# Single-tile slots by column parts, and the ranking and scores of the last tiles in another order

## The chip, the cores and the metric

The kernel runs on one core of a Trainium2 chip. The metric is the device time of one execution in microseconds (us). Matrix products run on TensorE (PE in the profile; PEld is its weight load), element-wise work on VectorE (DVE), ScalarE (ACT) and GpSimd (POOL), and SyncE (SP) issues most transfers. Each engine works through its own queue in order; between queues, an instruction waits for the semaphores of those whose data or buffers it needs.

## The reference

All in float32, with random inputs of fixed sizes:

```python
def _attn_ref(r, k, v, w, u):            # B 2, H 8, S 768, D 48
    for t in range(S):
        cur = np.einsum('bhd,bhe->bhde', u[None] * kt, vt)
        y[:, :, t] = np.einsum('bhd,bhde->bhe', rt, state + cur)
        state = wt[:, :, :, None] * state + np.einsum('bhd,bhe->bhde', kt, vt)

def _moe_ref(x, w_gate, w1, w2):         # N 1536, D 384, E 8, F 1024
    P = np.exp(logits - logits.max())    # logits = x @ w_gate
    for _ in range(8):
        P /= P.sum(1, keepdims=True) + 1e-09
        P /= P.sum(0, keepdims=True) + 1e-09
        P *= N / E
    for e in range(E):
        out += P[:, e:e + 1] * (np.maximum(x @ w1[e], 0.0) @ w2[e])

def _moe2_ref(x, expert_emb, tau, w1, w2):   # same sizes
    logits = normalised(x) @ normalised(expert_emb).T / tau
    expert_idx = np.argmax(logits, axis=1)
    gate_w = softmax(logits)[np.arange(N), expert_idx]
    for e in range(E):
        mask = expert_idx == e
        out[mask] = gate_w[mask, None] * (np.maximum(x[mask] @ w1[e], 0.0) @ w2[e])

def reference(**kwargs):
    x = rows of _attn_ref                # 1536 rows of 384
    return _moe2_ref(x=_moe_ref(x=x, **moe), **moe2)
```

## The kernel before

The 1536 rows are 12 tiles of 128. Each float32 product is made of three matmuls of rounded operands (high by high, high by low, low by high); `hh` and `hl` are the high and low half of a hidden value, and a weight split (`wA`, `wB`) takes ScalarE for the high half (L252) and VectorE for the low half (L258).

The work goes in stages: the recurrence (to about 100 us), the first mixture with eight experts on all rows (to about 870 us), and the top-1 mixture in slots, each of which takes the rows of one expert (up to two tiles of 128, gathered from a table `xs` in memory into which each row was scattered), to about 1035 us. The last expert of the first mixture runs in four units of three tiles, `m1_unit(E - 1, 0/3/6/9)`. A unit is a list of pieces: eight hidden pieces (nine matmuls, L274) and then product pieces (L294 to L296). Behind each piece the lists given to `run` put side work, so the position in a list sets the place in every engine's queue. There is no planner behind it: what is issued later stands later in the queue.

The side work of these units prepares the top-1 mixture. As the add L804 (`acc`) finishes a tile's row, ScalarE copies it to PSUM (L885) and sums its squares (L877, `sumsq`), VectorE makes five of the eight scores (`route_dots`, L731: a product with accumulated sum and a read of that sum), and GpSimd and ScalarE make the others (L738, L724). Then, for groups of tiles (`route`): the one-hot of the best expert (`route_arg`, L916 to L921), the root chain for the norm (`gate_a`, L817 to L832), positions within the expert (`route_pos`: L935 matmuls on TensorE, then L937 to L944), running counts (`route_cum`, `cum`, L951), the gate (`gate_b`, `gate_c`, L975 to L988), and the scatter (`route_rows`, L958). Tiles 10 and 11 get their scores on TensorE instead, by transposes of the finished row (`route_tr`, L893) and matmuls (`route_mm`, L904). `choose` takes the fullest expert after three tiles for slot 0; `order` (L1010 on), after nine tiles, ranks the other experts into slots 1 to 7.

Ten slots (`m2_slot`) follow, the last ones for what does not fit. Slots 3, 5 and 7 (`TURN`) hold one tile, and their hidden pieces run turned: `turned_pieces` takes the rows as stationary operand, makes the hidden values of all 1024 columns in three slabs over the contraction into three banks, and transposes them (L341) for the second product. The second tile of every slot from the first on stands under a condition on a bit of a word. While one slot runs, the splits of the next slot's weights stand in its side work (`its`, `at_`), and `m2_xT(s + 1)` transposes the next slot's gathered rows (L707).

Of the kernel before, what the change touches and what calls it, by code (L numbers as in the profile page):

```python
# [8 lines left out]
F32 = mybir.dt.float32  # L9
# [10 lines left out]
def rwkv_sinkhorn_moe_top1_moe(  # L20
# [291 lines left out]
    def turned_pieces(g, xh, xl, finish, own=False):  # L312


        w1h, w1l, _, _ = wt[g]
        parts = [range(0, 3), range(3, 6), range(6, 8)]
        hts, box, banks, hid = [], [], [], []

        def slab(kk):
            if kk == 0:  # L320
                banks.extend(ps() for _ in parts)
            mm = [(xh, w1h), (xh, w1l), (xl, w1h)]
            for i, (a, b) in enumerate(mm):
                for p, fs in zip(banks, parts):
                    n = len(fs) * 128
                    cs = slice(fs[0] * 128, fs[0] * 128 + n)
                    nc.tensor.matmul(
                        p[:, 0:n], a[:, kk, :], b[:, kk, cs],
                        start=(kk == 0 and i == 0), stop=(kk == KD - 1 and i == 2),
                    )  # L330
            if kk == KD - 1:
                for i, fs in enumerate(parts):
                    n = len(fs) * 128
                    hid.append(hp.tile([128, 384], F32, tag="hh", name="hid") if own else acc[:, 8 + i])
                    nc.scalar.activation(out=hid[i][:, 0:n], in_=banks[i][:, 0:n], func=AF.Relu)

        def turn(i):
            t, n = ps(), len(parts[i]) * 128
            for q in range(len(parts[i])):
                cs = slice(q * 128, (q + 1) * 128)  # L340
                nc.tensor.transpose(t[:, cs], hid[i][:, cs], ident)  # L341
            hh = hp.tile([128, 384], F32R, tag="hh", name="hh")
            hl = hp.tile([128, 384], F32R, tag="hl", name="hl")
            nc.scalar.activation(out=hh[:, 0:n], in_=t[:, 0:n], func=AF.Copy)  # L344
            nc.vector.tensor_tensor(out=hl[:, 0:n], in0=t[:, 0:n], in1=hh[:, 0:n].bitcast(F32), op=ALU.subtract)
            for q in range(len(parts[i])):
                cs = slice(q * 128, (q + 1) * 128)
                hts.append((hh[:, cs], hl[:, cs]))

        return [lambda k=k: slab(k) for k in range(KD)] + [lambda i=i: turn(i) for i in range(3)] + [  # L350
            lambda q=q: y_part(g, q, 4, 0, hts, box) for q in range(3)
        ] + [lambda: finish(0, y_part(g, 3, 4, 0, hts, box))]

    S_t = {}
    B21, B22, B31, B32, B11, T3, T1, T2, T4 = range(9)
# [525 lines left out]
    def route_dots(t, es, n_pool):  # L881
        x = acc[:, t, 0:DM]
        if es[0] == 0:
            xp, junk = rr["xp", t] = ps(), ps()
            nc.scalar.activation(out=xp[:, 0:DM], in_=x, func=AF.Copy)  # L885
            sumsq(t, junk)
        dots(lg[:, t, :], x, *rr["xp", t], lambda e: en[:, e, :], es, n_pool, late)

    def route_tr(t):
        x1 = acc[:, t, 0:DM]  # L890
# [104 lines left out]
    def choose():  # L995
# [8 lines left out]
        nc.vector.tensor_copy(first, est[:, 0:1])  # L1004
        nc.vector.tensor_scalar(oe, wdesc, m, None, op0=ALU.is_equal)

    def order():
# [8 lines left out]
        nc.vector.tensor_scalar(mk, kio, est[:, 0:1], full, op0=ALU.is_ge, op1=ALU.mult)  # L1016
        b = small[0].tile([128, NS], F32, tag="b", name="b")
        nc.vector.tensor_tensor(b, kio, mk, ALU.add)
        nc.vector.tensor_scalar(ids[:, E - 1:E], est[:, 0:1], 0.0, None, op0=ALU.add)
        nf = sp.tile([128, E], F32, tag="fl", name="nf")  # L1020
        nc.vector.tensor_scalar(nf[:, 0:1], full, -1.0, 1.0, op0=ALU.mult, op1=ALU.add)
        nc.vector.tensor_scalar_add(nf[:, 1:2], est[:, 0:1], -float(E - 1))
        nc.vector.scalar_tensor_tensor(
            out=b[:, E:E + 1], in0=nf[:, 1:2], scalar=nf[:, 0:1], in1=b[:, E:E + 1], op0=ALU.mult, op1=ALU.add
        )

        key = sp.tile([128, E], F32, tag="jk", name="key")
        nc.vector.scalar_tensor_tensor(out=key, in0=p, scalar=float(E), in1=wdesc, op0=ALU.mult, op1=ALU.add)
        nc.vector.scalar_tensor_tensor(out=key, in0=oe, scalar=float(OOB), in1=key, op0=ALU.mult, op1=ALU.add)
        sq = [128, E, E]  # L1030
        c = sp.tile([128, NTILE, E], F32, tag="tmp", name="rank")[:, 0:E]
        nc.vector.tensor_tensor(
            c, key.unsqueeze(1).to_broadcast(sq), key.unsqueeze(2).to_broadcast(sq), ALU.is_gt
        )
        nc.vector.tensor_reduce(f, c, axis=AX.X, op=ALU.add)
        se = [128, E - 1, E]
        d = c[:, 0:E - 1]
        c = sp.tile([128, NTILE, E], F32, tag="tl", name="at")[:, 0:E - 1]
        nc.vector.tensor_tensor(
            c, f.unsqueeze(1).to_broadcast(se), want.unsqueeze(2).to_broadcast(se), ALU.is_equal  # L1040
        )
        nc.vector.tensor_tensor(d, c, wdesc.unsqueeze(1).to_broadcast(se), ALU.mult)
        nc.vector.tensor_reduce(b[:, 1:E], d, axis=AX.X, op=ALU.add)
        nc.vector.tensor_scalar(b[:, 1:E], b[:, 1:E], -1.0, float(E), op0=ALU.mult, op1=ALU.add)
        nc.vector.tensor_scalar_min(blk, b, float(E + NOV - 1))
        nc.vector.tensor_tensor(c, c, pow2.unsqueeze(2).to_broadcast(se), ALU.mult)
        nc.vector.tensor_reduce(wtab, c.rearrange("p s e -> p e s"), axis=AX.X, op=ALU.add)
        nc.vector.tensor_scalar_mul(nf[:, 0:1], nf[:, 0:1], float(1 << E))
        nc.vector.scalar_tensor_tensor(out=wtab, in0=oe, scalar=nf[:, 0:1], in1=wtab, op0=ALU.mult, op1=ALU.add)
# [154 lines left out]
    with tc.manual_schedule():  # L1204
# [156 lines left out]

        def m2_slot(s, extra=()):
            its = w_items(E + s + 1)
            turned = s in TURN
            side = [[] for _ in range(KF + 8)]
            if s and s + 2 < NS:
                side[0].append(lambda: m2_load(s + 2))
            if s and s + 1 < NS:
                side[2].append(lambda: m2_xT(s + 1))
            if s == 1:  # L1370
                side[0].append(overflow_word)
                side[KF + 1].append(overflow_rows)
# [1 line left out]
                for i, j in enumerate((3, 5, 7)):  # L1374
                    side[j].append(lambda t=3 * (s - 2) + i: over_scatter(t))
            if turned:
                its = its[KD:]
                at_ = (0, 1, 3, 5)
            elif s + 1 in TURN:
                its = its + w_items(E + s + 2)[:KD]  # L1380
                at_ = (0, 1, 3, 4, 5, 6, 7, KF, KF + 1, KF + 1)
            else:
                at_ = (5, 6, 7, 8, 9, 15, 15) if s == 0 else (1, 4, 6, KF, KF, KF + 1, KF + 1)
            if its:
                for j, it in zip(at_, its):
                    side[j].append(it)
# [3 lines left out]
            if s == 0:  # L1390
                run(pieces, side)
                return
            n = 10 if turned else KF + 2
            run(pieces[:n], side)
            if s == 1:
                word.append(nc.values_load(word_t[0:1, 0:1], min_val=0, max_val=(NS + 1) * (1 << NS) - 1))
            with tc.If(((word[0] >> s) & 1) > 0):
                for pc in pieces[n:]:
                    pc()

# [43 lines left out]
        def load_to(g):  # L1444
# [95 lines left out]
```

## Time and profile before

| | |
|---|---|
| median of 3 runs | 1045.8 us (1045.76 to 1046.46) |
| profiled execution | 1045.61 us, span 1043.9 us |
| mean granted TensorE clock | 0.993 |
| busy: TensorE, weight load | 1015.2 us (97%), 995.0 us (95%) |
| busy: VectorE, ScalarE, GpSimd | 700.9 us (67%), 413.9 us (40%), 207.1 us (20%) |

The span runs from the first to the last instruction; the profiled execution's time also holds what lies around it. With TensorE busy for 97%, an idle stretch on it is time that the program loses, and an idle stretch elsewhere is not, unless TensorE waits for that engine.

### The profile page before, as it was taken

What the parts mean: (1) busy time and instruction counts of PE and PEld (TensorE: products, weight loads), DVE (VectorE), ACT (ScalarE), POOL (GpSimd) and SP (SyncE); (2) the same over time, 40 slices, a digit from 0 to 9 for tenths busy, and PEclk for the clock granted to TensorE, in tenths of its full rate; (3) what the DMA queues carried; (4) which work ended last, traced back from release to release, by engine and by line L of the source; (5) the groups of instructions that cost most, each with busy time, mean ns of one, the idle gap of its engine ahead of it and who ended that gap; (6) DMA issues with size and microseconds to landing.
All of it is one profiled execution on the core that took longest, in us unless ns stands there. A gap on an engine that the chain in (4) does not pass through costs nothing.

```text
span 1043.9 us, 19767 instructions
## 1 busy us (share of the span) xinstructions
PE 1015.2 (97%) x7714; PEld 995.0 (95%) x7714; DVE 700.9 (67%) x1413; ACT 413.9 (40%) x851; POOL 207.1 (20%) x393
## 2 busy tenths in 40 slices
PE   7999999999999999999999999999999998999996
PEld 6899999999999999999999999999999997999996
DVE  7998858666655665566456556655547787977764
ACT  3323234535432342333234323433434545566553
POOL 3211152040100010002001000000234663144101
PEclk9999999999999999999999999999999999999998
DMA  8435201201220122021011100120011314888762
GB/s 248 120 109 158 84 10 46 76 1 31 84 78 1 61 84 77 10 88 50 7 31 61 31 1 31 61 77 15 19 59 37 100 38 139 293 300 281 244 207 68
DMA packets 55783, 91.71 MB, mean 88 GB/s; under 512 B 5355, under 2 KB 47191, under 8 KB 55554
## 3 DMA queue, kind: packets, MB, share of 16 engines
q1 hardware_dynamic: 53056, 85.60, 26.4%
q0 software_dynamic: 2624, 4.75, 1.2%
q8 instruction: 64, 1.05, 0.4%
q14 instruction: 37, 0.30, 0.1%
q10 hardware_dynamic: 2, 0.00, 0.0%
HBM read 80.42 MB, written 13.28 MB: 90 GB/s over the span
## 4 chain that ended last, share of the span: by engine, by line
PE 67%; issue 14%; DVE 9%; POOL 5%; ACT 2%; DMA 1%; POOLq 0%; DVEq 0%; SPq 0%; ACTq 0%
PE ps L502 29%; PE ps L427 24%; PE ps L274 6%; PE ps L294 2%; PE ps L296 2%; PE ps L295 1%; POOL tmp L738 1%; DVE ps L731 1%; POOL xs L1136 1%; PE ps L631 1%; POOL out_dram L1182 1%; DVE hl L443 1%; DVE keep L438 1%; PE ps L663 1%; ACT hh L442 1%
## 5 line engine op out<-in xcount | busy, mean ns | idle before, releaser
L502 PE MATMUL ps<-wA,hh 128*128 128x384 f32 x864 | 221.6, 337 | 0.4 <-ACT hh L442 0.4
L502 PEld LDWEIGHTS ps<-wA,hh 128*128 128x128 f32 x864 | 156.7, 188 | 1.2 <-ACT hh L442 1.2
L506 DVE SCALAR_TENSOR_TENSOR acc<-ps,Pe,acc 128x384 f32<-128x384 f32 x144 | 88.7, 616 | 101.7 <-PE ps L502 101.3
L433 ACT ACTIVATE keep<-ps 128x384 f32<-128x384 f32 x144 | 70.2, 488 | 208.9 <-PE ps L427 207.1
L502 PE MATMUL ps<-wA,hl 128*128 128x384 f32 x432 | 145.6, 337 | 0.2
L443 DVE SCALAR_TENSOR_TENSOR hl<-keep,hh 128x384 fp32r<-128x384 f32 x144 | 81.7, 567 | 92.0 <-ACT hh L442 92.0
L438 DVE TENSOR_TENSOR keep<-ps,keep 128x384 f32<-128x384 f32 x192 | 106.3, 554 | 40.2 <-PE ps L427 34.2
L232 POOL TENSOR_TENSOR stage<-stage 128x128 f32<-128x128 f32 x96 | 49.3, 535 | 416.4 <-DMA stage<-in_moe_w_dram 414.5
L442 ACT ACTIVATE hh<-keep 128x384 fp32r<-128x384 f32 x144 | 75.4, 524 | 123.8 <-DVE keep L438 123.6
L427 PE MATMUL ps<-xTAhi,wA 128*128 128x384 f32 x396 | 101.6, 338 | 0.2 <-ACT keep L433 0.2
L279 ACT ACTIVATE hh<-ps 128x256 fp32r<-128x256 f32 (+1 forms) x128 | 53.0, 416 | 91.5 <-PE ps L274 72.9
L294 PE MATMUL ps<-wA,hh 128*128 128x384 f32 x248 | 85.1, 343 | 1.8 <-ACT hh L344 1.7
L296 PE MATMUL ps<-wA,hl 128*128 128x384 f32 x248 | 83.6, 337 | 0.4
L295 PE MATMUL ps<-wA,hh 128*128 128x384 f32 x248 | 83.3, 336 | 0.0
L502 PEld LDWEIGHTS ps<-wA,hl 128*128 128x128 f32 x432 | 81.1, 188 | 1.2 <-DVE hl L443 1.2
L258 DVE TENSOR_TENSOR wA<-stage,wA 128x768 fp32r<-128x768 f32 (+2 forms) x65 | 72.5, 1118 | 4.9 <-ACT wA L252 4.6
L280 DVE SCALAR_TENSOR_TENSOR hl<-ps,hh 128x256 fp32r<-128x256 f32 (+1 forms) x128 | 57.5, 460 | 26.6 <-ACT hh L279 26.2
L502 PE MATMUL ps<-slot,hh 128*128 128x384 f32 x288 | 74.2, 339 | 0.0
L427 PEld LDWEIGHTS ps<-xTAhi,wA 128*128 128x128 f32 x396 | 71.7, 188 | 0.5 <-ACT keep L433 0.5
L252 ACT ACTIVATE wA<-stage 128x768 fp32r<-128x768 f32 (+2 forms) x65 | 60.5, 956 | 26.6 <-POOL stage L232 26.0
L427 PE MATMUL ps<-xTAlo,wA 128*128 128x384 f32 x198 | 66.7, 337 | 0.0
L274 PE MATMUL ps<-xTAhi,wA 128*128 128x256 f32 (+1 forms) x336 | 58.3, 309 | 0.0
(332 smaller groups left out, 2093.1 us busy)
## 6 DMA issues: line engine op xcount, KB each, us to landing
stage<-in_moe_w_dram SPq DMA_DIRECT2D x55, 384.0 KB
stage<-in_moe_w_dram SPq DMA_DIRECT2D x19, 512.0 KB
en<-in_moe_w_dram SPq DMA_DIRECT2D x17, 512.0 KB
stage<-in_moe_w_dram SPq DMA_DIRECT2D x28, 256.0 KB
rkv<-in_rkv_dram SPq DMA_DIRECT2D x12, 576.0 KB
en<-in_moe_w_dram SPq DMA_DIRECT2D x18, 384.0 KB
rk<-in_wrk_dram SPq DMA_DIRECT2D x24, 192.0 KB
stage<-in_moe_w_dram SPq DMA_DIRECT2D x28, 128.0 KB
```

Of the source, the lines that this page charges most:

```text
L258: eng.tensor_tensor(out=lo, in0=src, in1=hi.bitcast(F32), op=ALU.subtract)
L274: nc.tensor.matmul(p[:, 0:n], w1_of(g, kk, f)[lo], b[:, kk, :], start=(i == 0), stop=(i == len(mm) - 1))
L294: nc.tensor.matmul(p, hh[:, ts], w2h, start=(f == 0), stop=False)
L295: nc.tensor.matmul(p, hh[:, ts], w2l, start=False, stop=False)
L296: nc.tensor.matmul(p, hl[:, ts], w2h, start=False, stop=(f == KF - 1))
L427: nc.tensor.matmul(t, w, x, start=first_mm and q == 0, stop=q == n - 1, skip_group_check=True,)
L433: nc.scalar.activation(out=t, in_=st_[i][bank][:, 0:384], func=AF.Copy)
L438: nc.vector.tensor_tensor(t, st_[i][bank][:, 0:384], t, ALU.add)
L442: nc.scalar.activation(out=hh, in_=src, func=AF.Relu)
L443: nc.vector.scalar_tensor_tensor(out=hl, in0=src, scalar=0.0, in1=hh.bitcast(F32), op0=ALU.max, op1=ALU.subtract)
L502: nc.tensor.matmul(p, h[:, ts], w, start=n == 0, stop=n == len(mm) - 1)
L506: nc.vector.scalar_tensor_tensor(out=a, in0=p, scalar=P[:, t, e:e + 1], in1=a, op0=ALU.mult, op1=ALU.add)
```

## The change

Five edits, in the diff below.

1. In the single-tile slots, `part(i)` makes the hidden columns of one part with all nine matmuls of the contraction, and the list becomes part 0, part 1, transposes 0, part 2, transposes 1, product 0, transposes 2, products 1 to 3. The two first weight splits in the slot (`pre`) are issued ahead of the pieces, two more at pieces 2 and 6, and the next slot's row transposes behind piece 5.
2. `sumsq` of a tile is issued behind the tile's last scores.
3. The ranking is split: `rank_a`, `rank_b` and `rank_c` (counts of the first six tiles, keys, ranks, tables) stand in the third unit at sides 6, 7 and 9; what is left in `order` is ten instructions.
4. In the third and fourth units: the scatters of tiles 3 to 5 stand behind the scores of tile 6, two weight splits move into slot 0, the add of tile 10 comes between the scores of tile 9, and the root chain of tiles 10 and 11 is on GpSimd. In slot 0 the steps of tiles 10 and 11 spread over pieces 1 to 6 and the next splits come a piece later.
5. The condition is `word & (1 << s)` instead of `(word >> s) & 1`.

```diff
+        def part(i):
+            p, fs = ps(), parts[i]
+            n = len(fs) * 128
+            cs = slice(fs[0] * 128, fs[0] * 128 + n)
+            mm = [(a, b, kk) for a, b in ((xh, w1h), (xh, w1l), (xl, w1h)) for kk in range(KD)]
+            for q, (a, b, kk) in enumerate(mm):
+                nc.tensor.matmul(p[:, 0:n], a[:, kk, :], b[:, kk, cs], start=(q == 0), stop=(q == len(mm) - 1))
+            hid.append(hp.tile([128, 384], F32, tag="hh", name="hid"))
+            nc.scalar.activation(out=hid[i][:, 0:n], in_=p[:, 0:n], func=AF.Relu)
...
-        return [lambda k=k: slab(k) for k in range(KD)] + [lambda i=i: turn(i) for i in range(3)] + [
-            lambda q=q: y_part(g, q, 4, 0, hts, box) for q in range(3)
-        ] + [lambda: finish(0, y_part(g, 3, 4, 0, hts, box))]
+        if own:
+            pa = [lambda i=i: part(i) for i in range(3)]
+            return [pa[0], pa[1], ts[0], pa[2], ts[1], ys[0], ts[2]] + ys[1:]
+        return [lambda k=k: slab(k) for k in range(KD)] + ts + ys
...
-            sumsq(t, junk)
         dots(lg[:, t, :], x, *rr["xp", t], lambda e: en[:, e, :], es, n_pool, late)
+        if es[-1] == E - 1:
+            sumsq(t, rr["xp", t][1])
...
+    def rank_a():
+        p = counts()
+        key = rr["key"] = small[0].tile([128, E], F32, tag="sc1", name="key")
+        nc.vector.scalar_tensor_tensor(out=key, in0=p, scalar=float(E), in1=wdesc, op0=ALU.mult, op1=ALU.add)
+        nc.vector.scalar_tensor_tensor(out=key, in0=oe, scalar=float(OOB), in1=key, op0=ALU.mult, op1=ALU.add)
+        sq = [128, E, E]
+        p = rr["rank"] = ps()
+        c = p[:, 0:E * E].rearrange("p (a b) -> p a b", b=E)
+        nc.vector.tensor_tensor(
+            c, key.unsqueeze(1).to_broadcast(sq), key.unsqueeze(2).to_broadcast(sq), ALU.is_gt
+        )
+        nc.vector.tensor_reduce(key, c, axis=AX.X, op=ALU.add)
...
             if s and s + 1 < NS:
-                side[2].append(lambda: m2_xT(s + 1))
+                side[5 if turned else 2].append(lambda: m2_xT(s + 1))
...
             if turned:
-                its = its[KD:]
-                at_ = (0, 1, 3, 5)
+                its, pre = its[KD + 2:], its[KD:KD + 2]
+                at_ = (2, 6)
...
-                at_ = (5, 6, 7, 8, 9, 15, 15) if s == 0 else (1, 4, 6, KF, KF, KF + 1, KF + 1)
+                at_ = (6, 7, 8, 9, 10, 15, 15) if s == 0 else (1, 4, 6, KF, KF, KF + 1, KF + 1)
...
-            with tc.If(((word[0] >> s) & 1) > 0):
+            with tc.If((word[0] & (1 << s)) > 0):
...
-            dt[0:1], dt[1:2], dt[2:3], rt[0:2], its[1:2], [], [rt[2]], [rt[3]],
-            its[2:3], rt[4:], dots_of(6), its[3:4], dots_of(7), its[4:5],
+            dt[0:1], dt[1:2], dt[2:3], rt[0:2], its[1:2], [], [rt[2], rank_a], [rt[3], rank_b],
+            its[2:3], [rt[4], rank_c], dots_of(6), its[3:4] + [rt[5]], dots_of(7), its[4:5],
...
-        ra, rb = route(8, 10, nc.gpsimd), route(10, 12, nc.vector)
+        ra, rb = route(8, 10, nc.gpsimd), route(10, 12, nc.gpsimd)
...
-            [order, lambda: load_to(E + SURE)], its[5:6], [], [], dots_of(9)[0:2], dots_of(9)[2:], [ra[1]], [ra[0]],
+            [order, lambda: load_to(E + SURE)], [], [], [], dots_of(9)[0:1], [], [], dots_of(9)[1:] + [ra[1], ra[0]],
...
-            (0, [lambda: route_mm(10), lambda: route_tr(11), ra[4], more_stages]), (1, [lambda: route_mm(11), ra[5], rb[0], rb[1]] + its[6:7]),
-            (3, rb[2:4]), (4, rb[4:]), (5, [lambda: m2_load(1)]), (6, [lambda: m2_load(2)]),
+            (0, [lambda: route_mm(10), lambda: route_tr(11), ra[4], more_stages]),
+            (1, [lambda: route_mm(11), ra[5], rb[1], rb[0]]), (2, its[5:6]),
+            (3, rb[2:3]), (4, its[6:7]), (5, rb[3:4]), (6, rb[4:] + [lambda: m2_load(1)]), (7, [lambda: m2_load(2)]),
```

TensorE in the third unit, before, at the end of the position matmuls of tiles 3 to 5 (L935) and the eighth hidden piece (L274):

```order
L935 MATMUL ps<-oh,oneb 128x8
L935 LDWEIGHTS oneb
L935 MATMUL ps<-oh,oneb 128x8
L935 LDWEIGHTS oneb
L935 MATMUL ps<-cum,oneb 128x8
L274 MATMUL ps<-xTAhi,wA 128x384 x6
L274 MATMUL ps<-xTAlo,wA 128x384 x3
L294 MATMUL ps<-wA,hh 128x384
```

The same place after the change, where line numbers are higher by 15 (L950 are the position matmuls, L1007 the counts):

```order
L950 MATMUL ps<-oh,oneb 128x8
L950 LDWEIGHTS oneb
L950 MATMUL ps<-oh,oneb 128x8
L950 LDWEIGHTS oneb
L950 MATMUL ps<-cum,oneb 128x8
L1007 LDWEIGHTS oneb
L1007 MATMUL ps<-cum,oneb 128x8
L274 MATMUL ps<-xTAhi,wA 128x384 x6
L274 MATMUL ps<-xTAlo,wA 128x384 x3
L294 MATMUL ps<-wA,hh 128x384
```

One matmul of `cum` and its weight load stand new between the last position matmul and the hidden piece.

VectorE in the same unit, before, from the position steps (L937) to the gate (L976):

```order
L937 TENSOR_SCALAR lm<-s_149 128x3
L941 TENSOR_TENSOR pr<-ps,oh 128x24
L942 TENSOR_REDUCE pos<-pr 128x3
L943 TENSOR_TENSOR lm<-pos,lm 128x3
L944 SCALAR_TENSOR_TENSOR pidx<-lm,pos 128x3
L951 TENSOR_TENSOR cum<-cum,oh 128x8 x3
L280 SCALAR_TENSOR_TENSOR hl<-ps,hh 128x384
L975 RECIPROCAL nrm_y<-nrm_y 128x3
L976 TENSOR_TENSOR lg<-lg,nrm_y 128x24
```

After, where `key` is made from the counts:

```order
L952 TENSOR_SCALAR lm<-s_149 128x3
L956 TENSOR_TENSOR pr<-ps,oh 128x24
L957 TENSOR_REDUCE pos<-pr 128x3
L958 TENSOR_TENSOR lm<-pos,lm 128x3
L959 SCALAR_TENSOR_TENSOR pidx<-lm,pos 128x3
L966 TENSOR_TENSOR cum<-cum,oh 128x8 x3
L1025 SCALAR_TENSOR_TENSOR key<-ps,wdesc 128x8
L1026 SCALAR_TENSOR_TENSOR key<-oe,key 128x8
L1030 TENSOR_TENSOR ps<-key 128x64
L1033 TENSOR_REDUCE key<-ps 128x8
L280 SCALAR_TENSOR_TENSOR hl<-ps,hh 128x384
```

Four instructions of `rank_a` stand between the running counts and the lower half of the eighth hidden value.

VectorE in the fourth unit, before, from the add of tile 9 (L804), through the scores (L731), to the add of tile 10:

```order
L804 SCALAR_TENSOR_TENSOR acc<-ps,Pe,acc 128x384
L731 ISA ps,lg<-ps,en 128x384
L731 ISA lg 128x1
L731 ISA ps,lg<-ps,en 128x384
L731 ISA lg 128x1
L731 ISA ps,lg<-ps,en 128x384
L731 ISA lg 128x1
L731 ISA ps,lg<-ps,en 128x384
L731 ISA lg 128x1
L731 ISA ps,lg<-ps,en 128x384
L731 ISA lg 128x1
L804 SCALAR_TENSOR_TENSOR acc<-ps,Pe,acc 128x384
```

After (L818 are the adds, L745 the scores; the row ahead is the last of `order`):

```order
L1070 SCALAR_TENSOR_TENSOR wtab<-oe,sc_9536,wtab 128x8
L818 SCALAR_TENSOR_TENSOR acc<-ps,Pe,acc 128x384
L745 ISA ps,lg<-ps,en 128x384
L745 ISA lg 128x1
L745 ISA ps,lg<-ps,en 128x384
L745 ISA lg 128x1
L818 SCALAR_TENSOR_TENSOR acc<-ps,Pe,acc 128x384
L745 ISA ps,lg<-ps,en 128x384
L745 ISA lg 128x1
L745 ISA ps,lg<-ps,en 128x384
L745 ISA lg 128x1
L745 ISA ps,lg<-ps,en 128x384
```

The add of tile 10 moved from behind five scores to behind two, and the split that stood ahead of the add of tile 9 is gone.

TensorE in slot 3, before, from the last slab (L327) over the next slot's row transposes (L707) and the hidden transposes (L341) to the products:

```order
L327 MATMUL ps<-wA,shi_9313 128x384 x2
L327 MATMUL ps<-wA,shi_9313 128x256
L327 MATMUL ps<-wA,slo_9315 128x384 x2
L327 MATMUL ps<-wA,slo_9315 128x256
L707 MATMUL ps<-ident,rows_9309 128x128 x6
L341 MATMUL ps<-ident,hid 128x128 x8
L294 MATMUL ps<-wA,hh 128x384
L295 MATMUL ps<-wA,hh 128x384
L296 MATMUL ps<-wA,hl 128x384
```

After, the whole way from the first part (L343), over transposes (L351), to the first product:

```order
L343 MATMUL ps<-wA,shi_9329 128x384 x6
L343 MATMUL ps<-wA,slo_9331 128x384 x3
L343 MATMUL ps<-wA,shi_9329 128x384 x6
L343 MATMUL ps<-wA,slo_9331 128x384 x3
L351 MATMUL ps<-ident,hid 128x128 x3
L343 MATMUL ps<-wA,shi_9329 128x256 x6
L343 MATMUL ps<-wA,slo_9331 128x256 x3
L351 MATMUL ps<-ident,hid 128x128 x3
L294 MATMUL ps<-wA,hh 128x384
L295 MATMUL ps<-wA,hh 128x384
L296 MATMUL ps<-wA,hl 128x384
L294 MATMUL ps<-wA,hh 128x384
```

The transposes of the first part stand ahead of the third part's matmuls, and the first product follows the second transposes.

## Rows read from the trace of the kernel before

**Rows 1.** Waits of TensorE from 800 us: us in total, times, longest

```profile
PE ps L893 <- DVE acc L804: 2.8, 1, 2.8
PE ps L274 <- DVEq L1397: 2.1, 3, 0.7
PE ps L294 <- ACT hh L344: 1.7, 3, 0.6
PE ps L274 <- DVE lg L731: 0.7, 1, 0.7
PE ps L296 <- DVE hl L280: 0.7, 1, 0.7
PE ps L707 <- DMA rows<-xs: 0.4, 1, 0.4
```

**Rows 2.** Windows: us, busy by engine (x), PEclk, DMA share, GB/s; below, TensorE alone

```profile
850.00:875.00 25.00, 22.19 (x153) 20.97 (x152) 19.77 (x80) 10.15 (x32) 10.96 (x24) 0.93 0.37 121
...
869.20:872.40 3.20, 3.20 (x22) 0.51 0.69 235
```

**Rows 3.** Timeline of TensorE, slot 3: start, length, then idle before and releaser

```profile
934.46 0.44 PE L294 MATMUL ps<-wA,hh 128*128 128x384 f32 x1 [0.57 <-ACT hh L344]
934.74 0.33 PE L295 MATMUL ps<-wA,hh 128*128 128x384 f32 x1
935.22 0.45 PE L296 MATMUL ps<-wA,hl 128*128 128x384 f32 x1
```

**Rows 4.** Timeline of VectorE, fourth unit: the order step and the add behind

```profile
856.37 0.15 DVE L1012 TENSOR_TENSOR sc<-ps,oe 128x8 f32<-128x8 f32 x1
...
857.67 1.55 DVE L1023 SCALAR_TENSOR_TENSOR b<-nf,b 128x1 f32<-128x1 f32 x1
...
861.68 0.23 DVE L1049 SCALAR_TENSOR_TENSOR wtab<-oe,nf,wtab 128x8 f32<-128x8 f32 x1
861.83 0.95 DVE L258 TENSOR_TENSOR wB<-stage,wB 128x768 fp32r<-128x768 f32 x1
...
864.40 0.57 DVE L731 CUSTOM_DVE_ANT_0 ps<-ps,en 128x384 f32<-128x384 f32 x1 [1.10 <-ACT ps L877]
...
867.52 0.61 DVE L804 SCALAR_TENSOR_TENSOR acc<-ps,Pe,acc 128x384 f32<-128x384 f32 x1
```

**Rows 5.** Timeline of TensorE, third unit: the eighth hidden piece

```profile
825.01 1.30 PE L274 MATMUL ps<-xTAhi,wA 128*128 128x384 f32 x6
```

**Rows 6.** Timeline of VectorE, third unit, scores to running counts

```profile
814.23 0.57 DVE L731 CUSTOM_DVE_ANT_0 ps<-ps,en 128x384 f32<-128x384 f32 x1 [3.38 <-ACT ps L877]
...
817.88 1.22 DVE L258 TENSOR_TENSOR wB<-stage,wB 128x1024 fp32r<-128x1024 f32 x1
...
823.15 0.55 DVE L280 SCALAR_TENSOR_TENSOR hl<-ps,hh 128x384 fp32r<-128x384 f32 x1
...
824.47 0.18 DVE L921 TENSOR_TENSOR oh<-wdesc,s 128x24 bf16<-128x24 f32 x1
...
827.17 0.17 DVE L941 TENSOR_TENSOR pr<-ps,oh 128x24 f32<-128x24 f32 x1
...
827.87 0.55 DVE L951 TENSOR_TENSOR cum<-cum,oh 128x8 bf16<-128x8 bf16 x3
```

**Rows 7.** Timeline of ScalarE, third unit: square, split, hidden value

```profile
813.60 0.48 ACT L877 ACTIVATE ps<-acc 128x384 f32<-128x384 f32 x1
...
816.36 1.04 ACT L252 ACTIVATE wB<-stage 128x1024 fp32r<-128x1024 f32 x1
...
822.47 0.47 ACT L279 ACTIVATE hh<-ps 128x384 fp32r<-128x384 f32 x1
```

**Rows 8.** Timeline of GpSimd: first and last root-chain instruction, a scatter

```profile
867.00 0.22 POOL L817 TENSOR_SCALAR ssq<-ssq 128x2 f32<-128x2 f32 x1
...
871.19 0.24 POOL L832 TENSOR_SCALAR nrm_y<-nrm_y 128x2 f32<-128x2 f32 x1
...
883.74 0.98 POOL L958 DMA_INDIRECT xs<-acc,pidx  x1 [7.23 <-DVE acc L988]
```

More of the change, by code (lines that the diff above doesn't have):

```diff
@@ L333, in slab @@
                     n = len(fs) * 128
-                    hid.append(hp.tile([128, 384], F32, tag="hh", name="hid") if own else acc[:, 8 + i])
+                    hid.append(acc[:, 8 + i])
                     nc.scalar.activation(out=hid[i][:, 0:n], in_=banks[i][:, 0:n], func=AF.Relu)
+        def part(i):
[7 more added lines that the diff above has]
+            nc.scalar.activation(out=hid[i][:, 0:n], in_=p[:, 0:n], func=AF.Relu)
         def turn(i):
@@ L348, in turn @@
                 hts.append((hh[:, cs], hl[:, cs]))
-        return [lambda k=k: slab(k) for k in range(KD)] + [lambda i=i: turn(i) for i in range(3)] + [
-            lambda q=q: y_part(g, q, 4, 0, hts, box) for q in range(3)
-        ] + [lambda: finish(0, y_part(g, 3, 4, 0, hts, box))]
+        ys = [lambda q=q: y_part(g, q, 4, 0, hts, box) for q in range(3)]
+        ys.append(lambda: finish(0, y_part(g, 3, 4, 0, hts, box)))
+        ts = [lambda i=i: turn(i) for i in range(3)]
+        if own:
+            pa = [lambda i=i: part(i) for i in range(3)]
+            return [pa[0], pa[1], ts[0], pa[2], ts[1], ys[0], ts[2]] + ys[1:]
+        return [lambda k=k: slab(k) for k in range(KD)] + ts + ys
     S_t = {}
@@ L1005, in choose, with rank_b, rank_c @@
         nc.vector.tensor_scalar(oe, wdesc, m, None, op0=ALU.is_equal)
+    def rank_a():
[10 more added lines that the diff above has]
+        nc.vector.tensor_reduce(key, c, axis=AX.X, op=ALU.add)
+    def rank_b():
+        key, p, se = rr["key"], rr["rank"], [128, E - 1, E]
+        a, d = [p[:, o:o + (E - 1) * E].rearrange("p (a b) -> p a b", b=E) for o in (256, 0)]
+        nc.vector.tensor_tensor(
+            a, key.unsqueeze(1).to_broadcast(se), want.unsqueeze(2).to_broadcast(se), ALU.is_equal
+        )
+        nc.vector.tensor_tensor(d, a, wdesc.unsqueeze(1).to_broadcast(se), ALU.mult)
+        nc.vector.tensor_reduce(mk[:, 1:E], d, axis=AX.X, op=ALU.add)
+        nc.vector.tensor_scalar(blk[:, 1:E], mk[:, 1:E], -1.0, float(E), op0=ALU.mult, op1=ALU.add)
+    def rank_c():
+        a = rr["rank"][:, 256:256 + (E - 1) * E].rearrange("p (a b) -> p a b", b=E)
+        nc.vector.tensor_tensor(a, a, pow2.unsqueeze(2).to_broadcast([128, E - 1, E]), ALU.mult)
+        nc.vector.tensor_reduce(wtab, a.rearrange("p s e -> p e s"), axis=AX.X, op=ALU.add)
+        nc.vector.tensor_scalar(ids[:, E - 1:E], est[:, 0:1], 0.0, None, op0=ALU.add)
+        nc.vector.tensor_scalar_add(mk[:, 0:1], est[:, 0:1], -float(E - 1))
     def order():
@@ L1015, in order @@
         nc.vector.tensor_single_scalar(full, full, float(CAP), op=ALU.is_ge)
[L1016 to L1021, printed above, removed]
@@ L1022, in order @@
-        nc.vector.tensor_scalar_add(nf[:, 1:2], est[:, 0:1], -float(E - 1))
+        nc.vector.tensor_scalar(f[:, 0:1], full, -1.0, 1.0, op0=ALU.mult, op1=ALU.add)
+        b = small[0].tile([128, NS - E], F32, tag="b", name="b")
+        nc.vector.tensor_scalar(mk[:, E:NS], kio[:, E:NS], est[:, 0:1], full, op0=ALU.is_ge, op1=ALU.mult)
+        nc.vector.tensor_tensor(b, kio[:, E:NS], mk[:, E:NS], ALU.add)
         nc.vector.scalar_tensor_tensor(
-            out=b[:, E:E + 1], in0=nf[:, 1:2], scalar=nf[:, 0:1], in1=b[:, E:E + 1], op0=ALU.mult, op1=ALU.add
+            out=b[:, 0:1], in0=mk[:, 0:1], scalar=f[:, 0:1], in1=b[:, 0:1], op0=ALU.mult, op1=ALU.add
@@ L1025, in order @@
         )
[L1027 to L1049, printed above, removed]
+        nc.vector.tensor_scalar_min(blk[:, E:NS], b, float(E + NOV - 1))
@@ L1051, in overflow @@
+        nc.vector.tensor_scalar_mul(f[:, 0:1], f[:, 0:1], float(1 << E))
+        nc.vector.scalar_tensor_tensor(out=wtab, in0=oe, scalar=f[:, 0:1], in1=wtab, op0=ALU.mult, op1=ALU.add)
     def overflow():
@@ L1363, in m2_slot @@
             its = w_items(E + s + 1)
-            turned = s in TURN
+            turned, pre = s in TURN, []
             side = [[] for _ in range(KF + 8)]
@@ L1393, in m2_slot @@
             n = 10 if turned else KF + 2
+            for it in pre:
+                it()
             run(pieces[:n], side)
```

## The prediction

> **What bounds the kernel now.** I read the page's busy times first: TensorE is busy 1015.2 of the 1043.9 us span, so what can be won without removing matmuls is its idle time. Then the waits of TensorE from 800 us on [rows 1]: 2.8 us for the sum of tile 10 on VectorE, 2.1 us in three waits of 0.71 at slot ends, 1.7 us in three waits for the rounded hidden values of the turned slots, 0.7 us for a score, 0.7 us for a lower half and 0.4 us for a row load: 8.4 us. Outside this, TensorE idles only while the program starts and ends, where the change does nothing. The windows then show that the 2.8 us wait costs more than itself: the granted clock is 0.51 in the 3.20 us that follow 869.2, that is 1.2 in place of 2.4 GHz [rows 2]. Matmuls at half rate take twice as long, so half of the 3.2 us is lost: 1.6. So waits and their aftermath in reach make about 10 us, one per cent of the time, and the change is worth what it takes of these, less what it adds.
>
> **The change part by part.** Sums start from the profiled execution, 1045.61 us, which lies 0.2 below the median of the runs, 1045.8.
>
> *Turned slots.* Hidden columns now come in three parts of nine matmuls, and the transposes and the products stand in between. Matmul columns are the same. The wait of 0.57 for the first rounded transposed part goes [rows 1], since between that part's transposes and its use now stand a whole part of 9 matmuls x 256 columns and three transposes; a further 0.14 before a lower half goes as well (the third product starts at 935.22, where the end of the one before it, 934.74 + 0.33, gives 935.07) [rows 3]. Added are two more changes between transposes and matmuls, which I price at 0.08 each (an estimate, three quarters of the difference) by the 0.44 that the first product after transposes takes, against 0.33 for the second [rows 3]. 0.57 + 0.14 - 0.16 = 0.55, in three slots -1.65. The wait of 0.71 at the end of these slots stays: the next slot's first piece still waits for VectorE's scaling of the last product, at the same distance. The weight splits put first are the same splits on the same two engines; at 928 us these are ahead of TensorE by more than a piece, so I put them at nothing. If that cover were gone, they cost the first part one split, 0.9.
>
> *Scores, adds, ranking near the end of the last expert.* The piece at 844 waited 0.73 for the last of five scores in a row [rows 1]; with the sums of squares behind the scores and the ranking out of the way it is no longer last: -0.73. The wait of 2.81 at 865 goes back to a full VectorE queue: the order step stands there from 856.37 to 861.9, 22 instructions, 5.5 us, and behind it a split, an add and five scores, until the add of tile 10 at 867.52 ends at 868.1 [rows 4]. Twelve of the 22 leave, the split of 0.95 leaves, three of five scores are put behind the add; the one slow instruction of 1.55 stays, with nine small ones of 0.2: 3.3 [rows 4]. The add of tile 10 then comes 5.5 - 3.3 + 0.95 + 3 x 0.62 (five scores take 864.40 to 867.52) = 5.0 us earlier by VectorE's own work. In the new program, with the delay of the next paragraph, I get it at 868.6 for a need at 871.7. So the wait goes, -2.81, and its half clock, -1.6, with a margin of about 3 us.
>
> *The first portion of the ranking.* This adds a matmul of counts on TensorE right behind the position matmuls of tiles 3 to 5, ahead of the eighth hidden piece. It reads the running counts that VectorE makes out of those very position matmuls. So it is a new wait on the bound engine, with all the rest of the unit queued behind. In the trace TensorE is through the position matmuls at 825.01 and starts the eighth piece at once [rows 5]. VectorE is then not waiting for anything: its queue runs without idle from 814.23, and the position steps, with a split and two lower halves ahead of them, begin at 827.17, the three running counts end at 828.42 [rows 6]. By this the counts matmul waits 3.4 us: the lower bound, if nothing else moved. But the sums of squares moved too. ScalarE now does that of tile 4 behind VectorE's scores of that tile, and ahead of its upper half of wB, which was at 816.36 [rows 7]: VectorE's half of the split begins some 0.6 later than 817.88. And that of tile 5 comes behind the last score at 823.15 + 0.6, ahead of the hidden value that ran at 822.47 [rows 7], so that the next lower half comes at 824.9 for 823.15: 1.75 late. All that follows on VectorE is back to back, so the one-hot at 824.47 and the running counts are late by this too: 828.42 + 1.75 + 0.2 (two passings between engines) = 830.4. TensorE then idles first for the one-hot, then for the counts, 830.4 - 825.0 = 5.4 in all. I take 5.4 of 3.4 to 5.7. The twelve instructions of the three portions that follow lie on VectorE while it has room.
>
> A wait of this size is what dropped the clock at 865. The row: 2.81 idle, then 0.51 granted for 3.2 us [rows 2]. I take the same, +1.6; bounds 0 (the idle time is here in two portions with matmuls between) and 3.2 (both portions drop it). The Trainium skill, in "TensorE: Matmul & The Clock Gate", section "What's actually happening", calls the low rate the default state, which activity releases, and has the moment of the switch vary by itself and not with the kernel. By that rule the drop could come or not after the same wait, and the term be 0 in some executions and the sum 1044.4. The one drop in this trace agrees that a wait can cost the full rate; that it may also not is shown by no run here.
>
> *Slot 0.* A lower half waited 0.67 behind weight splits [rows 1]; the splits come a piece later: -0.67. The root chain of tiles 10 and 11 goes to GpSimd: 16 instructions, 4.4 us for such a chain in the row of tiles 8 and 9 [rows 8], and more than on VectorE. It is not itself last, but its later steps are spread over pieces 3, 5 and 6, where they were 3 and 4: the scatter at 883.74 [rows 8] comes some two pieces of 1.05 later. From that scatter to the matmul that waited for the rows there are 7.1 us (883.74 to 890.85, the 0.4 of [rows 1]). TensorE comes there later as well, by 5.4 + 1.6 - 0.73 - 2.81 - 1.6 - 0.67 = 1.2. The wait grows by 2.1 - 1.2 = +0.9; bounds 0 and 2.1.
>
> *The condition* loses one register instruction; no row shows a cost of it on TensorE beyond the 0.71, I take 0.
>
> Sum: -1.65 - 0.73 - 2.81 - 1.6 - 0.67 = -7.46; +5.4 + 1.6 + 0.9 = +7.9; net +0.44. 1045.61 + 0.44 = 1046.05. Forecast 1046.0: gains and the new wait cancel. What can be told from no change is 0.2%, 2.1 us.
>
> **The rivals.** *A: the new wait is short.* The counts wait only the 3.4, since VectorE's extra delay is taken up somewhere, and the clock stays: -7.46 + 3.4 + 0.9 = -3.2, 1042.4. For it: the row of tile 4's scores can start 0.5 earlier, because the square of 0.48 no longer stands between copy and scores [rows 7]. Against: no idle time on VectorE in 14 us to take it up. At the far end, with no wait at all, -7.46 + 0.9 gives 1039.0; it needs VectorE 3.4 us ahead of where it is.
>
> *B, slower: the transposes of tile 10 still wait.* The late VectorE queue of 830 is not worked off, the add of tile 10 is late at 871.7 by as much as before, and 2.81 + 1.6 come back: 1046.0 + 4.4 = 1050.4. It decides from the point where VectorE lags more than the margin of 3 us in the last unit. For it: VectorE is busy 19.8 of 25 us there [rows 2], and 12 new instructions come in at 830 to 838. Against: VectorE idled 1.1 before these scores even so [rows 4]. A half of this gives 1048.2; so does a clock that drops twice, +1.6.
>
> *C: the turned slots gain nothing*, because the products come to wait for their lower halves behind the splits: 1046.0 + 1.65 = 1047.7, still within 0.2%.
>
> **How the numbers follow.** Forecast with its own range 1044 to 1048: 0.46 (C in it with 0.1). A: 0.33, its far end 0.06 of that. B and its halves, or the clock twice: 0.21. Faster by over 0.2%, below 1043.7: A, and a little of the forecast's edge, 0.35. Slower, above 1047.9: 0.21. Same: 0.44. The range leaves out A's far end and B whole: 1041.3 to 1048.8.
>
> **What would show it.** A wait of TensorE of about 3.5 us at the new counts matmul, after one of about 2 at the position matmuls, some 825 to 831 us, and a granted clock near 0.5 in a stretch behind it; no wait at the tile 10 transposes, none at the last unit's score; row load wait of slot 1 about 1.3; turned slots 0.55 shorter each, with the 0.71 still there. The prediction is wrong if the counts matmul waits under 2 us (then far faster), or if tile 10 still waits (slower).

## The result, and the profile after

The changed kernel takes 1055.2 us (1053.74 to 1056.89, 4 runs) beside 1046.13 (1045.76 to 1047.27, 4 runs) of the kernel before: 1.0085 times, interval 1.0068 to 1.0103. It is slower by 9 us, where I forecast no change and a range that ended at 1048.8. The profiled execution takes 1055.67, its span is 1054.0.

Waits of TensorE from 800 us on, after (the wait, total us, times, longest), to be held against [rows 1]:

```profile
PE ps L1007 <- DVE cum L966: 3.3, 1, 3.3
PE ps L721 <- DMA rows<-xs: 3.2, 1, 3.2
PE ps L950 <- DVE oh L936: 2.5, 1, 2.5
PE ps L274 <- DVEq L1420: 2.1, 3, 0.7
PE ps L274 <- DVE lg L745: 1.5, 1, 1.5
PE ps L294 <- ACT hh L279: 0.8, 1, 0.8
PE ps L296 <- DVE hl L280: 0.7, 1, 0.7
PE ps L919 <- ACT xT L910: 0.6, 1, 0.6
PE ps L950 <- ACT hh L279: 0.4, 1, 0.4
```

Gone are the 2.8 for the add of tile 10 and the 1.7 in the turned slots. New are 3.3 at the counts matmul, 2.5 ahead of it at the position matmuls, and 3.2 in place of 0.4 for the rows of slot 1; the score wait doubled instead of going, and there are small waits for hidden values. The timeline of TensorE at the first two, after (start, length, operation, idle before), answers to [rows 5]:

```profile
829.19 0.17 PE L950 MATMUL ps<-oh,ub 128*128 128x8 bf16 x1 [2.54 <-DVE oh L936]
...
832.98 0.17 PE L1007 MATMUL ps<-cum,oneb 128*128 128x8 bf16 x1 [3.35 <-DVE cum L966]
833.01 2.27 PE L274 MATMUL ps<-xTAhi,wA 128*128 128x384 f32 x6
```

From 826.7 to 833 us TensorE does the position matmuls and nothing else, and the six matmuls behind take 2.27 us where they took 1.30. The clock granted, third column from the right, before DMA share and GB/s:

```profile
833.00:834.50 1.50, 1.50 (x6) 0.50 0.26 95
...
838.00:840.00 2.00, 2.00 (x12) 0.89 0.00 0
```

The 0.89 of the last window puts the return to full rate at about 838.4, so TensorE works at half rate for 5.4 us. Why the one-hot was late stands on ScalarE (L891 is now the square, L899 the copy, L279 a hidden value) in the same unit, after, answering to [rows 7]:

```profile
819.51 0.50 ACT L891 ACTIVATE ps<-acc 128x384 f32<-128x384 f32 x1 [1.02 <-DVE lg L745]
...
820.04 1.04 ACT L252 ACTIVATE wB<-stage 128x1024 fp32r<-128x1024 f32 x1
...
826.57 0.49 ACT L891 ACTIVATE ps<-acc 128x384 f32<-128x384 f32 x1 [2.43 <-DVE lg L745]
...
827.09 0.47 ACT L279 ACTIVATE hh<-ps 128x384 fp32r<-128x384 f32 x1
```

The two squares wait 1.02 and 2.43 us for VectorE's last score of their tile, and behind them stand a weight split and a hidden value that wait for nothing of the kind. VectorE, after, answering to [rows 6]:

```profile
821.11 1.23 DVE L258 TENSOR_TENSOR wB<-stage,wB 128x1024 fp32r<-128x1024 f32 x1 [1.17 <-ACT wB L252]
...
827.59 0.56 DVE L280 SCALAR_TENSOR_TENSOR hl<-ps,hh 128x384 fp32r<-128x384 f32 x1 [1.06 <-ACT hh L279]
...
828.96 0.18 DVE L936 TENSOR_TENSOR oh<-wdesc,s 128x24 bf16<-128x24 f32 x1
...
831.65 0.17 DVE L956 TENSOR_TENSOR pr<-ps,oh 128x24 f32<-128x24 f32 x1
...
832.38 0.55 DVE L966 TENSOR_TENSOR cum<-cum,oh 128x8 bf16<-128x8 bf16 x3
```

VectorE, which had no idle in this stretch before, idles 1.17 for the split and 1.06 for the hidden value. These are the two late squares come back to it. The one-hot starts at 828.96 for 824.47: 4.5 late, of which 2.0 lie already ahead of this stretch (first row of the table below) and 2.5 are new. In the next unit ScalarE's squares wait for last scores again (4.34, 1.84 and 1.39 us), and TensorE waits 1.51 for a score and 0.83 for a hidden value.

Where the time went, as the difference of start times of the same instructions in the two traces of TensorE:

| place | after less before, us | step |
|---|---|---|
| first position matmuls of the last expert (799) | +2.0 | +2.0 |
| one-hot and counts waits (825) | +8.0 | +6.0 |
| half clock behind (839) | +10.5 | +2.5 |
| score, position matmuls, hidden values (845 to 858) | +13.1 | +2.7 |
| tile 10 transposes, and their half clock (868 to 873) | +8.7 | -4.4 |
| slot 0 (874) | +9.4 | +0.7 |
| rows of slot 1 (891) | +12.2 | +2.8 |
| half clock behind (893) | +13.8 | +1.6 |
| three turned slots (to 1000) | +10.2 | -3.6 |

The first step cannot be put down to the change. It arises in the first 110 us, and in the ten profiled executions of the changed kernel and of the experiments it lies between -0.3 and +2.0 at this place, though several of them hold the same code up to there; the changed kernel's own +2.0 is the largest. What it was in the executions without a profile is not known. So 8.1 of the 10.1 us between the two spans are left for the change.

The turned slot 3, after, answering to [rows 3] (L343 hidden parts, L351 transposes):

```profile
944.71 0.49 PE L351 MATMUL ps<-ident,hid 128*128 128x128 f32 x3
944.96 0.95 PE L343 MATMUL ps<-wA,shi 128*128 128x256 f32 x6
...
946.10 0.49 PE L351 MATMUL ps<-ident,hid 128*128 128x128 f32 x3
946.34 0.42 PE L294 MATMUL ps<-wA,hh 128*128 128x384 f32 x1
...
948.12 0.38 PE L351 MATMUL ps<-ident,hid 128*128 128x128 f32 x2
948.26 0.42 PE L294 MATMUL ps<-wA,hh 128*128 128x384 f32 x1
...
952.37 0.86 PE L274 MATMUL ps<-shi,wB 128*128 128x256 f32 x5 [0.71 <-DVEq L1420]
```

There is no wait at the first products; the 0.71 at the next slot's first piece stays.

### The profile page after: what moved, and what is told of

It is laid out like the page before. It is cut to its first block, busy times and chain, and to the rows that moved or that the text cites. A ratio compares the mean times of both kernels' runs of the same rounds, so it can differ in the third digit from the quotient of the medians.

```text
span 1054.0 us, 19727 instructions
## 1 busy us (share of the span) xinstructions
PE 1017.3 (97%) x7715; PEld 998.6 (95%) x7715; DVE 703.4 (67%) x1400; ACT 414.2 (39%) x851; POOL 208.3 (20%) x409
## 4 chain that ended last, share of the span: by engine, by line
PE 68%; issue 12%; DVE 10%; POOL 4%; ACT 3%; DMA 2%; POOLq 0%; SPq 0%; DVEq 0%; ACTq 0%
PE ps L516 28%; PE ps L441 24%; PE ps L274 6%; DVE ps L745 2%; PE ps L294 2%; PE ps L296 2%; PE ps L295 2%; POOL out_dram L1203 1%; POOL xs L1157 1%; DVE hl L280 1%; PE ps L645 1%; DMA stage<-in_moe_w_dram 1%; DVE hl L457 1%; DVE keep L452 1%; DVE wB L258 1%
## 5 line engine op out<-in xcount | busy, mean ns | idle before, releaser
L279 ACT ACTIVATE hh<-ps 128x256 fp32r<-128x256 f32 (+1 forms) x128 | 52.8, 415 | 91.2 <-PE ps L274 88.1
L274 PE MATMUL ps<-xTAhi,wA 128*128 128x256 f32 (+1 forms) x336 | 59.2, 312 | 0.0
```

The lines of the kernel that those rows point to most:

```text
L274: nc.tensor.matmul(p[:, 0:n], w1_of(g, kk, f)[lo], b[:, kk, :], start=(i == 0), stop=(i == len(mm) - 1))
```

## The experiments

My theory after the result had three places, to be taken away one by one: the counts matmul, the squares behind the scores, and the late scatter that the rows of slot 1 hang on. The rival was a VectorE queue that is full anyway, so that a wait removed in one place comes back in the next.

**Ranking portions later.** Line numbers are each run's own: from here on those of the changed kernel, or one lower, and in the squares alone those of the kernel before, one higher.

```diff
-            ..., [rt[2], rank_a], [rt[3], rank_b],
-            its[2:3], [rt[4], rank_c], dots_of(6), ...
+            ..., [rt[2]], [rt[3]],
+            its[2:3] + [rank_a], [rt[4], rank_b], dots_of(6) + [rank_c], ...
```

> The changed kernel with the three portions of the ranking two to one pieces later (sides 8, 9 and 10 of the third unit in place of 6, 7 and 9), so that a product piece stands between the position matmuls and the counts. Theory (the counts matmul holds TensorE for VectorE's running counts, 3.35 us, and the half clock behind it costs another 2.2): 1055.2 - 3.35 - 2.2 = about 1049.6, the wait at the counts gone, the wait of 2.5 at the position matmuls still there. Rival (VectorE's late queue is the cost, wherever TensorE meets it): the wait moves to the product pieces or to the next position matmuls, and the time stays within 1 us of 1055.

Measured 1047.8 us (1046.5 to 1049.41), ratio to before 1.0024 (1.0014 to 1.0035): 7.4 below the changed kernel. The counts wait went and did not come back; waits of TensorE in this run:

```profile
PE ps L950 <- DVE oh L936: 2.5, 1, 2.5
...
PE ps L274 <- DVE lg L745: 0.2, 1, 0.2
```

The wait of 2.5 for the one-hot alone still drops the clock: the granted clock is 0.50 from 828 to 830 us. The gain is 1.8 more than I expected. In the profiled executions 1.8 of it lies in the first 110 us (+0.2 over the kernel before, for +2.0 in the changed kernel). Behind that the counts wait gave 3.5, the half clock only 0.8 of the 2.2, and the score wait, which fell from 1.5 to 0.2, another 1.3: the portions at their new place are out of its way.

**Squares early.**

```diff
+            sumsq(t, junk)
         dots(lg[:, t, :], x, *rr["xp", t], lambda e: en[:, e, :], es, n_pool, late)
-        if es[-1] == E - 1:
-            sumsq(t, rr["xp", t][1])
```

> The changed kernel with the squares again ahead of the scores, all else as changed. Theory (the moved squares make ScalarE, and through it VectorE, late by some 2 us before the one-hot of tiles 3 to 5): the wait of 2.5 at the position matmuls shrinks below 1, later waits for scores shrink as well, 1052 to 1053.5; the counts wait stays at 3.4 or a little more. Rival (the squares cost nothing, VectorE is late by the ranking alone): 1055 within 1 us, the wait of 2.5 unchanged.

Measured 1046.39 (1044.36 to 1048.15), ratio 1.0002 (0.9991 to 1.0013): 8.8 below the changed kernel, far more than the theory's 2 to 3 (8.2 in the profiled executions, without the first 110 us). Its waits:

```profile
PE ps L1006 <- DVE cum L965: 3.3, 1, 3.3
PE ps L721 <- DMA rows<-xs: 3.3, 1, 3.3
PE ps L274 <- DVEq L1419: 2.1, 3, 0.7
PE ps L296 <- DVE hl L280: 0.7, 1, 0.7
```

All five waits in the two last units and at the start of slot 0 that are not for the counts are gone at once: one-hot, score, both hidden values, and the transposed rows (L919). So none of them is there without the squares behind the scores, and the counts wait of 3.3 is.

**Both.**

> Both edits: portions later and squares early. Theory: the effects add, 1046.5 to 1048, no wait over 1 us in the third unit; what is left over the kernel before is the row load of slot 1 (3.2, before 0.4) with its half clock, and the start. Rival (late queue): above 1050.

Measured 1041.31 (1039.73 to 1041.81), ratio 0.9956 (0.994 to 0.9973), faster than the kernel before, and better than the theory's 1046.5 to 1048, since each edit had given more by itself (7.4 and 8.8) than I had put down (5.6, and 2 to 3). 13.9 below the changed kernel, where the two edits alone sum to 16.2. The late start of the changed kernel may count in both: without the first 110 us the profiled executions give 6.0 and 8.2 alone and 13.0 together, so that little more than 1 us is shared; that this is the score wait, which either edit takes away, is likely but not shown. The rival (late queue) fails. The one big wait left is that for rows, the others are the three of 0.71 at slot ends and 0.7 for a lower half:

```profile
PE ps L721 <- DMA rows<-xs: 3.2, 1, 3.2
```

**Parts alone**, on the kernel before: edit 1 of the change and nothing else.

> The kernel before with the single-tile slots by parts alone (with the two splits first and the row transposes behind piece 5). Theory (the changed trace shows each of the three slots 1.1 to 1.2 shorter, and the start has nothing to do with them): 1046.1 - 3.5 = 1042.6. Rival 1 (my forecast of 0.55 a slot): 1044.4. Rival 2 (the 2.1 us that the changed kernel is late by already after 100 us comes with the new code of the turned pieces, which the first unit also runs): 1044.7, with the delay at the start in its trace.

Measured 1042.27 (1040.96 to 1045.54), ratio 0.9976 (0.9963 to 0.9989). The theory held: -3.6 us, 1.2 a slot, twice my 0.55. The trace shows the 3.5 in the three slots themselves. That the whole time agrees so well is in part luck: in the profiled execution the start is late by 0.95 and the row wait longer by 0.6, and against that the half clock behind the wait for tile 10 stayed away (see the last section).

**The squares alone**, on the kernel before, as in the change.

> The kernel before with the squares behind the scores and nothing else. Theory (the moved squares are a loss by themselves, some 6.5 as between the runs with later portions with and without them): 1051 to 1053, waits at position matmuls of 2.5 and at hidden values of the last unit. Rival 1 (my forecast's price, 1.75 late at the one-hot and nothing behind it): 1047.5 to 1048.5. Rival 2 (harmful only beside the ranking in portions): 1046.

Measured 1050.64 (1049.9 to 1052.64), ratio 1.0053 (1.0034 to 1.0073): a loss of 4.7 by itself, a little below the theory's 1051, above both rivals. Its waits are those that went with the squares early, but for the score:

```profile
PE ps L936 <- DVE oh L922: 2.5, 1, 2.5
...
PE ps L294 <- ACT hh L279: 0.8, 1, 0.8
PE ps L905 <- ACT xT L896: 0.8, 1, 0.8
...
PE ps L936 <- ACT hh L279: 0.4, 1, 0.4
PE ps L274 <- DVE lg L731: 0.2, 1, 0.2
```

The score wait is 0.2 here, for 0.7 before. So the squares by themselves shorten it, as the prediction had it, and its growth to 1.5 needs the squares and the ranking portions at their early place together.

**The row load**, three runs on the kernel with both edits. First the root chain back on VectorE, then on GpSimd ahead of the scatters of tiles 8 and 9 with the rest a piece earlier, then on VectorE with the gate and scatter at pieces 3 and 4:

```diff
+        ra, rb = route(8, 10, nc.gpsimd), route(10, 12, nc.vector)     # first and third
...
-            (1, [lambda: route_mm(11), ra[5], rb[1], rb[0]]), (2, its[5:6]),
-            (3, rb[2:3]), (4, its[6:7]), (5, rb[3:4]), (6, rb[4:] + [lambda: m2_load(1)]), ...
+            (1, [lambda: route_mm(11), rb[1], ra[5], rb[0]]), (2, its[5:6]),      # second
+            (3, rb[2:3]), (4, its[6:7] + rb[3:4]), (5, rb[4:] + [lambda: m2_load(1)]), (6, []), ...
...
+            (1, [lambda: route_mm(11), ra[5], rb[1], rb[0]]), (2, its[5:6]),      # third
+            (3, rb[2:4]), (4, rb[4:] + [lambda: m2_load(1)]), (5, its[6:7]), ...
```

> The kernel of the run before with both edits (portions later, squares early; 1041.3), and the root chain of tiles 10 and 11 on VectorE again, the spread over the pieces of slot 0 as in the changed kernel. Theory (the spread and VectorE's own queue set the last scatter; VectorE idled 2.0 for the chain on GpSimd, but the chain itself costs it 2.6): the row load of slot 1 is waited for as long as before, 2.5 to 3.8, 1041 to 1042. Rival (the chain on GpSimd, queued behind the scatters of tiles 8 and 9, sets it): wait below 1.5, 1038 to 1039.

> The same base, with the root chain of tiles 10 and 11 on GpSimd ahead of the scatters of tiles 8 and 9, and the gate, scatter and row load steps one piece earlier (4 and 5 in place of 5 and 6). Theory (the wait for the rows of slot 1 hangs on the last scatter): the scatter comes 3 to 4.5 earlier than 880.98, the rows land before TensorE asks for them, the 3.2 and the half clock behind it (1.3) go: 1036.8. Rival (the load is late by its queue and by the traffic of weights, not by the scatter): 1041 within 1.

> The same base, root chain on VectorE, gate at piece 3, scatter and load at piece 4, the last split of slot 0 at piece 5. Theory: scatter some 2 earlier, wait about 1 and no half clock behind it, 1037.5 to 1039; the three edits of the changed kernel that I did not undo (parts, add of tile 10 earlier, ranking in portions) are then worth 7 to 8 of the kernel before. Rival (VectorE has no room for the chain there, lower halves come late): waits for lower halves of over 1 in slot 0, 1041 or more.

Measured 1039.97 (1039.44 to 1043.19), ratio 0.9954 (0.994 to 0.9968); 1037.95 (1037.38 to 1039.15), 0.9931 (0.991 to 0.9952); 1039.05 (1038.7 to 1040.85), 0.9941 (0.9919 to 0.9964). The first is not clear of the run with both edits. Its row wait fell to 1.5, but not in the rival's way: its last two scatters start at 881.98 and 884.11, 1.0 later than with the chain on GpSimd, and TensorE comes 2.7 later itself, since it waited 1.8 for the one-hot of tiles 10 and 11 and ran at half rate behind. The last two scatters on GpSimd and the first load of rows on SyncE, in the run with both edits, and then the same in the second of the three:

```profile
880.98 1.92 POOL L972 DMA_INDIRECT xs<-acc,pidx  x1 [2.21 <-DVE acc L1002]
883.20 1.07 POOL L972 DMA_INDIRECT xs<-acc,pidx  x1 [0.30 <-issue]
```

```profile
885.92 0.39 SPq L1173 DMA_DIRECT2D rows<-xs  x1
```

```profile
878.13 1.68 POOL L972 DMA_INDIRECT xs<-acc,pidx  x1 [0.30 <-issue]
880.12 1.16 POOL L972 DMA_INDIRECT xs<-acc,pidx  x1 [0.30 <-issue]
```

```profile
882.93 0.39 SPq L1173 DMA_DIRECT2D rows<-xs  x1
```

TensorE takes up the rows at these times in the two runs:

```profile
889.17 0.84 PE L721 MATMUL ps<-ident,rows 128*128 128x128 f32 x6 [3.21 <-DMA rows<-xs]
```

```profile
886.14 0.85 PE L721 MATMUL ps<-ident,rows 128*128 128x128 f32 x6 [2.11 <-DMA rows<-xs]
```

The load is issued 1.65 us behind the end of the last scatter in both, and 3.2 us later TensorE goes on, so the wait hangs on the scatter and not on the traffic. The scatter came 2.9 earlier, a little less than the 3 to 4.5 expected, since four scatters now stand in a row. The wait is 2.1 and not gone, but no half clock follows it, and 3.4 are won of the 4.5 expected. As the chain's place and the steps' pieces were moved together, the run does not show which of the two brought the scatter forward. The third run has no row wait at all, but the 1.8 for the one-hot again, which the change had put behind the root chain: on VectorE that is 13 instructions.

**One-hot first**, on the third of these: `rb[0], rb[1]` for `rb[1], rb[0]`.

> The run with the root chain on VectorE and early gate (1039.05), with the one-hot of tiles 10 and 11 ahead of the root chain in VectorE's queue, as in the kernel before. Theory (the position matmuls of tiles 10 and 11 waited 1.8 for a one-hot that stood behind 13 instructions of the chain): that wait goes, 1039.05 - 1.8 = 1037.2, or up to 1 less if half clock went with it; the row wait of slot 1 may take some of it back, up to 1. Rival (VectorE's queue is full there, the wait moves to lower halves): 1039 within 0.5.

Measured 1038.25 (1038.05 to 1040.17), ratio 0.9941 (0.9928 to 0.9955); between the theory's 1037.2 and the rival's 1039, and not to be told apart from 1039.05. The wait for the one-hot went, and one for rows of 1.9 stands in its place (and 0.6 for a lower half), so here the pattern of the first rival holds, that a wait removed comes back elsewhere. 1037.95, 0.993 of the kernel before, is the lowest time, though not clear of 1038.25, and its remaining waits are 3 x 0.71 at slot ends and 2.1 for the rows.

## Why the prediction was wrong

*The counts wait* was right: its place, its cause and nearly its size (5.9 with the wait ahead of it, forecast 5.4 of 3.4 to 5.7). The half clock behind it cost 2.5 for my 1.6, in bounds.

*The moved squares* are the step that failed. I priced them as "1.75 late" at the one-hot, in one place, where they made it 2.5, and for the score at 844 I counted a gain: "it is no longer last: -0.73". The mechanism that I had named, ScalarE's later work behind VectorE's scores, acts at every tile with such scores: the two in this unit and the next ones too. So hidden values came late in the next unit as well, and with the ranking portions beside them the score wait grew to 1.5: +2.7 up to 858 us, where the sum had -0.7. Alone on the kernel before the squares cost 4.7, taken out of the changed kernel they give 8.8, against the 2 that I had for them.

*The row load* was mis-sized: +2.8 and a half clock of 1.6, for my 0.9. I had the scatter 2.1 later and TensorE 1.2; they came 11.2 and 9.4 later (894.90 for 883.74, and TensorE by the table). And the scatter's distance of 7.1 us to the matmul became 8.1 (894.90 to 903.05), as the first scatter takes 1.92 for 0.98; from the end of the second one it is 4.85 in both traces. I had the chain of GpSimd not limiting. By the trace it was, as VectorE after shows where it waits for the chain's last instruction (L846), which began behind two scatters:

```profile
892.72 0.17 DVE L990 RECIPROCAL nrm_y<-nrm_y 128x2 f32<-128x2 f32 x1 [1.99 <-POOL nrm_y L846]
```

The runs do not show what the chain's place costs by itself: back on VectorE it made the scatter no earlier. I had put no half clock behind this wait at all.

*Tile 10's wait* went as forecast, with its half clock: -4.4 for -4.4. That the half clock stood in the profiled execution of before was luck for this term, as the last section shows. Rival B, that the wait stays, did not come. *Slot 0* lost 0.7 where I had won 0.7: the wait for the lower half stayed (0.70), and 0.64 for transposed rows is new, which goes with the squares early. Of the two splits of edit 4, only one moves into slot 0 from the fourth unit; the other stood in slot 0 before, at piece 1. *Turned slots* gave 3.6 for 1.65: right mechanism, and a size that I took from waits alone. In the trace of before, the eight transposes in a row started at 932.86 and had themselves taken 1.03 us when the wait began (934.46 - 0.57 - 932.86); split in three they take 0.25, 0.24 and 0.14. The row of before:

```profile
932.86 1.04 PE L341 MATMUL ps<-ident,hid 128*128 128x128 f32 x8
```

No term stood for the start, where the profiled executions differ by 2.0; the prediction took the rest of the program as unchanged, and no run here shows what moves it. TensorE also waits 1.4 us in three places between 120 and 800 us, where the prediction has it idle only at the start and the end; as it does so in both traces, nothing follows from it here.

Rival A was wrong in what it supposed: nothing took up VectorE's delay.

## What to carry to other kernels

A wait put on an instruction delays all that stands behind it on that engine; when an instruction is moved behind another engine's result, price it at each place where the pattern occurs, and follow the queue behind it to the bound engine. Where two engines hand work to and fro, as ScalarE and VectorE do here, a wait in one comes back as idle time of the other, and a queue that had no idle time gets some. A bundle of edits can hold a gain and a loss at once: 3.6 us for the parts and, by the traces, up to 4.4 for tile 10 were in this one, and taking one of its edits back and putting another a piece or two later turned +9 us into -4.6. Scatter, add of tile 10 and condition were not tried alone.

## What was not expected of the hardware

The length of a wait does not tell alone whether half rate follows. The wait for tile 10 of the kernel before stands in the run with the parts alone too, at the same matmuls and nearly as long (2.77 for 2.81). Before, 0.51 was granted behind it [rows 2]. With the parts alone it was 1.00 (the matmul, then windows of TensorE behind it):

```profile
869.07 0.55 PE L907 MATMUL ps<-ident,acc 128*128 128x128 f32 x3 [2.77 <-DVE acc L818]
```

```profile
870.00:872.00 2.00, 2.00 (x23) 1.00 0.97 310
872.00:874.00 2.00, 2.00 (x28) 1.00 0.20 73
```

Windows behind a wait of 1.77 in the run with the chain on VectorE and the gate early (874.06 the first matmul behind it), and behind one of 1.87 in the run with the one-hot first (886.53):

```profile
876.00:878.00 2.00, 2.00 (x11) 0.50 0.72 195
878.00:880.00 2.00, 2.00 (x15) 0.72 0.00 2
```

```profile
886.50:888.00 1.50, 1.47 (x11) 1.00 0.92 310
```

The shorter one is followed by the 0.50, the longer one is not. Nor did it follow a wait of 2.11 (the row load with the chain ahead of the scatters) or one of 2.18 (tile 10 with the squares alone), while it followed those of 1.81, 2.5, 3.2 and 3.3 in the other traces. So what the trace of before alone could not show is shown: the 1.6 that such a wait costs may stay away, and what decides it these runs do not show. This agrees with the rule of the Trainium skill that the prediction weighed ("TensorE: Matmul & The Clock Gate", "What's actually happening"), by which the moment of the switch does not follow the kernel.
